# Fills in turned order, a narrow last pair, and a first k product in column halves

## The chip, the cores and the metric

The kernel runs on one core of a Trainium2 chip. A core has five engines that run side by side, each through its own list of instructions: PE (TensorE, matrix products), DVE (VectorE), ACT (ScalarE), POOL (GpSimd) and SP (SyncE, which here only issues transfers). They meet through semaphores. PE writes its products into PSUM, eight banks of 128 partitions by 512 float32 values; everything else lies in SBUF, 128 partitions wide. The metric is the device time of one execution in microseconds (us).

## What is computed

The reference is a transformer block on 2048 tokens of width 512, in float32:

```
h  = x + A(layernorm(x))
h2 = h + B(layernorm(h))

A: q, k, v = heads of x @ wqkv                         (32 heads of 16)
   phi(u)  = [softmax(u @ w_phi), softmax(-u @ w_phi)]
   o       = phi(q) (phi(k)^T v) / (phi(q) . sum(phi(k)) + 1e-6)
   A       = o @ wo
B: (token mixing) u = gelu(layernorm(h)^T @ w1 + b1)   (512 x 1792)
   B = (u @ w2 + b2)^T
```

Both layer norms are without weights; B normalizes its input once more, which the kernel folds into one scale.

## The kernel before

Every large product is made in a split form: an operand is rounded to the fast float32 form (the high part), the rest is the low part, and a product is high x high + high x low + low x high. ACT makes most high parts by a copy, DVE or POOL the low parts by a subtraction (`split`, lines 58 to 61). Tokens go in 16 tiles of 128.

**The beginning (lines 221 to 354)** has its order on PE, DVE, ACT and POOL written out by hand. The k, v and q weights arrive in chunks of 128 output columns: chunks 4 to 7 are k, 8 to 11 v, 0 to 3 q. `center` takes out the mean of a chunk, `fold` multiplies (or transposes) it on PE into PSUM, `hi_w` and `lo_w` (lines 279 to 287) copy it out as high and low part. `hi_w` runs on ACT, or on DVE where its second argument is True. `split_x(t)` makes the two parts of a token tile, the high one on ACT, the low one on POOL. Then `proj` (line 122) makes a tile's k logits in one PSUM bank: for tile 0 with `by_part`, all high x high first (four matmuls of 512 columns, one for each quarter of the contraction), then x low x weight high, then x high x weight low; for the other tiles in turn. DVE's `k_ops` reads the bank (the maximum of a head at line 154, the minimum at 155, the differences at 148 and 152). The centering of chunk 8 stands on DVE behind the low parts of chunks 4 to 7.

**The middle (lines 646 to 698)** runs 19 rounds `it`. A round carries different tiles at different steps: the denominators (POOL's `s_ez`, DVE's `s_den`, POOL's `s_pq` at line 463), the transposed q features (`s_tr`), the products with the k-v state in every second round (`s_num`, line 549), the product with `wo` (`s_wo`), the residual and the moments (`s_h`, `s_moments`), POOL's scale (`s_rstd`, lines 588 and 589) and the normalized tile `HN` with its parts (`s_hn`, line 593, `split` at 60 and 61). In even rounds `s_hn` makes tile `it - 4` near the beginning and tile `it - 3` at the end. `fills(it)` (line 640) already does part of B's first product: `fill(0)` adds tile `it - 5`, `fill(1)` tile `it - 6` to columns 0 to 255 and 256 to 511 of u, six matmuls each (lines 65 to 67). The w1 pairs for them are loaded, copied by ACT (line 612) and split by DVE (line 604) at the end of a round.

**The end (lines 752 to 912).** The rest of B's first product and gelu follow; then B's second product, in 8 pairs of token tiles by 7 steps `p`. A pair of tiles and a pair of contraction blocks make a 2 x 2 product of blocks, done with seven block products in place of eight; `PROD` (line 814) lists the seven: operand of w2, operand of u, PSUM bank, and half of the bank. With a half, `product` (line 818) writes 256 columns with three matmuls (high x high, high x low, low x high). With None it takes the bank whole: one matmul of 512 columns gives high x high in the left and high x low in the right half, and one of 256 adds low x high to the left. Steps 0 to 4 of a pair go step by step; the last two go product by product (`products(sp, [p - 1, p], order)`), so that the banks are complete one after the other. Then ACT and DVE combine the banks into two blocks of 128 x 512. For the last pair (`LAST`, lines 891 to 912) the two blocks, `hb`, are read back from `out`, b2 is added, and 14 DVE additions end in three stores: SP's whole first block, ACT's left and SP's right half of the second. w2 is loaded by SP, summed by DVE, copied by ACT (line 793) and split by DVE (line 802) in groups of two steps.

Tiles come from pools, and dependencies are kept by tile: a reader of a PSUM tile waits until the last matmul into it that precedes the reader in the program. A k or `py` tile is one bank. PE, DVE, ACT and POOL keep the written order in the first part and in the middle, PE, DVE and ACT at the end; between, a scheduler places the instructions.

Of the kernel before, what the change touches and what calls it, by code (L numbers as in the profile page):

```python
# [17 lines left out]
P = 128  # L18
S, D, H, DH, F = 2048, 512, 32, 16, 1792
NT = S // P  # L20
KD = D // P
NF = F // P
NP = NF // 2
HD = D // 2
# [6 lines left out]
LAG = 5  # L31
# [5 lines left out]
def block_kernel(ctx: ExitStack, tc: tile.TileContext, x, xT, wT, phic, wo, w1, b1, w2, b2,  # L37
                 kvmask, ident_in, out):
    nc = tc.nc
# [58 lines left out]
    X, XH, EQ, PK, VS, SQ, PS, W = {}, {}, {}, {}, {}, {}, {}, {}  # L98
# [23 lines left out]
    def proj(t, wh, wl, pool, name, by_part=False):  # L122
        o = pool.tile([P, D], F32, name=name, tag=name)
        if by_part:
            for i, (a, w) in enumerate(((0, wh), (1, wh), (0, wl))):
                for kt in range(KD):
                    nc.tensor.matmul(o, X[t][:, a, kt, :], w[:, kt, :], start=i == 0 and kt == 0,
                                     stop=i == 2 and kt == KD - 1)
            return o
        for kt in range(KD):  # L130
            mm3(o, X[t][:, 0, kt, :], X[t][:, 1, kt, :], wh[:, kt, :], wl[:, kt, :],
                kt == 0, kt == KD - 1)
        return o
# [87 lines left out]
    with tc.tile_pool(name="prep", bufs=1) as prep:  # L221
# [57 lines left out]
        def hi_w(c, vector=False):  # L279
            if vector:  # L280
                nc.vector.tensor_copy(parts(c)[0], FO[c])
            else:
                nc.scalar.activation(parts(c)[0], FO[c], AF.Copy)
# [8 lines left out]
        with tc.manual_schedule(engines={ET.PE, ET.DVE, ET.Activation, ET.Pool}):  # L292

            nc.gpsimd.tensor_mul(ph.rearrange("p c (a f) -> p c a f", f=DH),
                                 pc[:, 0:64].rearrange("p (c f) -> p c f", f=DH).unsqueeze(2).to_broadcast([P, 4, 8, DH]),
                                 pc[:, 64:72].unsqueeze(1).unsqueeze(3).to_broadcast([P, 4, 8, DH]))
            center(4, True)
            center(5, False)
            fold(4, ps_q, "pu")
            center(6, True)  # L300
            fold(5, ps_q, "pu")
            center(7, False)
            fold(6, ps_v, "pv")
            fold(7, ps_v, "pv")
            hi_w(4, True)
            hi_w(5, True)
            hi_w(6)
            split_x(0, xr[0])
            hi_w(7)
            for c in range(4, 8):  # L310
                lo_w(c)
            split_x(1, xr[1])
            k0 = proj(0, wkh, wkl, ps_k, "pk_ps", True)
            center(8, True)
            for c in range(9, 12):
                center(c, False)
            k1 = proj(1, wkh, wkl, ps_k, "pk_ps")
            for c in range(8, 12):
                fold(c, *((ps_q, "pu"), (ps_v, "pv"))[c // 10])
            k_ops(0, k0)  # L320
            split_x(2, xr[2])
            k_ops(1, k1)
            stats_x(0)
            k2 = proj(2, wkh, wkl, ps_k, "pk_ps")
            for c in range(8, 12):
                hi_w(c)
            for c in range(8, 12):
                lo_w(c)
            stats_x(1)
            exps(0, PK[0])  # L330
            split_x(3, xr[3])
            split_x(4, xr[4])
            v0 = proj(0, wvh, wvl, ps_v, "pv")
            k_ops(2, k2)
            stats_x(2)
            k3 = proj(3, wkh, wkl, ps_k, "pk_ps")
            k_norm(0)
            center(0, True)
            v_out(0, v0)
            exps(1, PK[1])  # L340
            center(1, False)
            exps(2, PK[2])
            v1 = proj(1, wvh, wvl, ps_v, "pv")
            k_ops(3, k3)
            fold(0, ps_q, "pu")
            fold(1, ps_q, "pu")
            k_norm(1)
            center(2, False)
            v_out(1, v1)
            hi_w(0)  # L350
            hi_w(1)
            lo_w(0)
            lo_w(1)
            center(3, False)
# [270 lines left out]
    def fill(p, pool=None):  # L625

        t = FN[p]
        FN[p] = t + 1
        if FL[p] <= t:
            fill_load(p)  # L630
        if any(part is WI[p, t - t % 2][1] for part, _, _ in LATER):
            flush()
        if t == 0:
            PU[p] = [pool.tile([P, D], F32, name="pu", tag="pu") for _ in range(2)]
        a, b = WI[p, t - t % 2]
        for c in range(2):
            mm3(PU[p][c], a[:, t % 2, c * P:(c + 1) * P], b[:, t % 2, c * P:(c + 1) * P],
                HN[t][:, 0], HN[t][:, 1], t == 0, t == NT - 1)

    def fills(it):  # L640
        if FN[0] <= it - LAG:
            fill(0, ps_f)
        if FN[1] < it - LAG:
            fill(1, ps_q)

    for it in range(NT + 3):
        even = it % 2 == 0
# [158 lines left out]
    with tc.issue_after(LO[-18]), tc.issue_after(LD[-20]):  # L806
        for i in range(3):
# [5 lines left out]

    PROD = ((2, 1, 0, None), (5, 5, 1, None), (0, 0, 2, 0), (1, 4, 2, 1), (3, 6, 3, None), (6, 2, 4, None),
            (4, 3, 5, None))
    LAST = PROD[:-1] + ((4, 3, 5, 0),)

    def product(o, half, a, b, first, start, stop):
        if half is None:
# [7 lines left out]
    def products(sp, ps, order):  # L827
        for a, b, bk, half in order:
            for p in ps:
                wh_, wl_ = AW[sp, p]  # L830
                product(bank[bk], half, (wh_[:, a], wl_[:, a]), UB[p, b], half != 1, p == 0, p == NP - 1)
# [6 lines left out]
    for n, (sp, p) in enumerate(STEPS):  # L838
# [10 lines left out]
                bank.append(pool.tile([P, 2, HD], F32, name="py", tag="pu"))  # L849
                n_bank += 1  # L850
        order = LAST if last else PROD
        if p < NP - 2:
            products(sp, [p], order)
            continue
        if p < NP - 1:
            continue
        products(sp, [p - 1, p], order)
        e = uo.tile([P, 2, HD], F32, name="e")
        u2 = uo.tile([P, HD], F32, name="u2", bufs=1)
        u3 = uo.tile([P, HD], F32, name="u3")  # L860
# [32 lines left out]
            nc.sync.dma_start(flat(hb[i]), out[(t + i) * P:(t + i + 1) * P, :])  # L893
            nc.vector.tensor_scalar(hb[i], hb[i], b2s[:, t + i:t + i + 1], None, op0=ALU.add)
        nc.scalar.activation(e[:, 1], bank[0][:, 0], AF.Copy)
        nc.vector.tensor_add(e[:, 1], bank[0][:, 1], e[:, 1])
        nc.vector.tensor_add(hb[1][:, 1], e[:, 1], hb[1][:, 1])
        nc.vector.tensor_sub(u2, bank[1][:, 0], e[:, 1])
        nc.vector.tensor_add(u2, bank[1][:, 1], u2)
        nc.vector.tensor_sub(hb[1][:, 0], hb[1][:, 0], u2)  # L900
        nc.vector.tensor_sub(u3, u2, bank[2][:, 0])
        nc.vector.tensor_sub(hb[1][:, 0], hb[1][:, 0], bank[2][:, 1])
        nc.vector.tensor_add(hb[0], hb[0], u3.unsqueeze(1).to_broadcast([P, 2, HD]))
        nc.vector.tensor_add(hb[0][:, 0], bank[2][:, 1], hb[0][:, 0])
        nc.vector.tensor_add(hb[0][:, 1], bank[3][:, 0], hb[0][:, 1])
        nc.vector.tensor_add(hb[0][:, 1], bank[3][:, 1], hb[0][:, 1])
        nc.sync.dma_start(out[t * P:(t + 1) * P, :], flat(hb[0]))
        nc.vector.tensor_add(hb[1][:, 0], bank[4][:, 0], hb[1][:, 0])
        nc.vector.tensor_add(hb[1][:, 0], bank[4][:, 1], hb[1][:, 0])
        nc.scalar.dma_start(out[(t + 1) * P:NT * P, 0:HD], hb[1][:, 0])  # L910
        nc.vector.tensor_add(hb[1][:, 1], bank[5][:, 0], hb[1][:, 1])
        nc.sync.dma_start(out[(t + 1) * P:NT * P, HD:D], hb[1][:, 1])


def _layout(A_x, A_wqkv, A_w_phi, A_wo, B_w1, B_b1, B_w2, B_b2):
# [46 lines left out]
```

## Time and profile before

| | |
|---|---|
| time, median of 3 runs | 529.30 us (529.26 to 529.55) |
| the profiled execution | 529.31 us, span 527.5 us, clock granted 0.999 |
| PE busy | 516.5 us, 98% of the span |
| DVE, ACT, POOL busy | 394.5, 278.3, 246.6 us |
| first instruction of the first k product | 9.92 us |
| stage with the fills | 172.6 to about 269 us |
| last matmul issued | 522.51 us |
| last store issued | 524.77 us |

A timeline row has the start, the duration, the engine and its line, the operation, out<-in, the shape, and in brackets the idle time of the engine before it and who ended it. PEld is PE's weight load, which overlaps its products; SPq and ACTq are issues of transfers. A matmul's duration is longer than the time after which the next one starts, so starts are what to compare. A row with x4 holds four instructions in a row. The list of waits has: who waited for whom, us in total, times, the longest. The chain is what ended last, followed back from the end; a row there has start, duration and what. A row of one line's instructions has the shortest, median and longest duration in ns.

### The profile page before, as it was taken

The page shows a single profiled execution, that of the slowest core. Times are in us where ns is not written, and L with a number is a line of the kernel's source. Part 1 is how long each engine was busy: PE and PEld are TensorE (multiplying, and loading weights), DVE is VectorE, ACT ScalarE, POOL GpSimd, SP SyncE. Part 2 cuts the span into 40 slices and gives each one's busy share as a digit, 9 for nine tenths or more (in the row PEclk, how much of TensorE's full clock was granted, in tenths as well). Part 3 has the DMA queues.
Part 4 walks back from the last instruction along what each step waited for, and adds up shares of the span by engine and source line. Part 5 has one row for each costly group of instructions (what it writes and reads, how often), then busy time and mean ns, then how long its engine had stood idle before and what let it go on. Part 6 is the DMA issues. An engine that isn't in the chain of part 4 may idle for free.

```text
span 527.5 us, 8840 instructions
## 1 busy us (share of the span) xinstructions
PE 516.5 (98%) x3343; PEld 434.1 (82%) x3343; DVE 394.5 (75%) x684; ACT 278.3 (53%) x481; POOL 246.6 (47%) x204
## 2 busy tenths in 40 slices
PE   8999999999999989999999999999999999999996
PEld 7888888887877767777788888888899999999995
DVE  6993999976899989875325523725779888988985
ACT  6999843534247776557746423625453434434430
POOL 2589699985999988887326000000002112111210
PEclk9999999999999999999999999999999999999999
DMA  8743310030122233334234354532215687668742
GB/s 298 203 129 121 84 39 21 1 86 18 49 93 80 91 96 115 109 111 139 85 99 119 99 161 155 166 98 80 69 51 113 160 187 169 135 146 198 141 61 60
DMA packets 36298, 58.52 MB, mean 111 GB/s; under 512 B 3744, under 2 KB 19360, under 8 KB 36256
## 3 DMA queue, kind: packets, MB, share of 16 engines
q1 hardware_dynamic: 31936, 51.37, 31.2%
q0 software_dynamic: 4032, 6.42, 9.6%
q8 instruction: 26, 0.43, 0.4%
q10 hardware_dynamic: 288, 0.17, 0.1%
q14 instruction: 16, 0.13, 0.1%
HBM read 46.81 MB, written 11.14 MB: 110 GB/s over the span
## 4 chain that ended last, share of the span: by engine, by line
PE 80%; POOL 12%; DVE 4%; ACT 2%; DMA 1%; issue 0%; DVEq 0%; POOLq 0%; ACTq 0%
PE py L820 12%; PE pu L65 11%; PE pu L66 10%; PE pu L67 10%; PE py L824 8%; PE py L821 6%; POOL ez L445 4%; POOL eq L463 3%; PE pv L66 3%; PE pv L67 3%; PE pv L65 3%; PE pk_ps L65 2%; PE pk_ps L67 2%; PE pk_ps L66 2%; POOL hs L61 2%; PE kvp L210 2%
## 5 line engine op out<-in xcount | busy, mean ns | idle before, releaser
L604 DVE TENSOR_TENSOR wlo<-wraw,whi 128x512 fp32r<-128x512 f32 x56 | 50.6, 908 | 54.6 <-ACT whi L612 53.4
L66 PE MATMUL pu<-hs,whi 128*128 128x512 f32 x224 | 87.6, 391 | 2.1 <-POOL hs L61 2.1
L65 PE MATMUL pu<-hs,whi 128*128 128x512 f32 x224 | 87.5, 395 | 0.0
L67 PE MATMUL pu<-hs,wlo 128*128 128x512 f32 x224 | 87.3, 390 | 0.0
L878 POOL DMA_DIRECT2D out<-ot x7 | 6.2, 889 | 149.1 <-DVE ot L874 149.1
L793 ACT ACTIVATE whi<-wraw 128x1792 fp32r<-128x1792 f32 x28 | 47.4, 1701 | 46.7 <-PE py L820 20.6
L820 PE MATMUL py<-uf,whi 128*128 128x512 f32 x195 | 70.9, 399 | 0.0
L802 DVE TENSOR_TENSOR wlo<-wraw,whi 128x1792 fp32r<-128x1792 f32 x28 | 56.5, 2022 | 12.0 <-PE py L821 8.9
L612 ACT ACTIVATE whi<-wraw 128x512 fp32r<-128x512 f32 x56 | 34.9, 626 | 47.3 <-PE pu L66 43.0
L821 PE MATMUL py<-uf,wlo 128*128 128x256 f32 x195 | 54.9, 282 | 0.0
L66 PEld LDWEIGHTS pu<-hs,whi 128*128 128x128 f32 x224 | 42.1, 188 | 11.5 <-POOL hs L61 3.1
L65 PEld LDWEIGHTS pu<-hs,whi 128*128 128x128 f32 x224 | 42.1, 188 | 10.8 <-issue 2.5
L67 PEld LDWEIGHTS pu<-hs,wlo 128*128 128x128 f32 x224 | 42.1, 188 | 9.0 <-DVE wlo L604 0.4
L820 PEld LDWEIGHTS py<-uf,whi 128*128 128x128 f32 x195 | 36.8, 189 | 7.3
L445 POOL TENSOR_TENSOR ez<-eq,zB 128x1024 f32<-128x1024 f32 x16 | 40.6, 2539 | 4.4 <-ACT zB L492 4.4
L821 PEld LDWEIGHTS py<-uf,wlo 128*128 128x128 f32 x195 | 36.9, 189 | 0.0
L198 POOL TENSOR_TENSOR pk<-pk,sk 128x1024 f32<-128x1024 f32 x16 | 31.0, 1943 | 7.9 <-DVE sk L197 5.3
L463 POOL TENSOR_TENSOR eq<-eq,w 128x1024 f32<-128x1024 f32 x16 | 31.9, 1997 | 1.2 <-DVE w L460 1.2
L824 PE MATMUL py<-uf,whi 128*128 128x256 f32 x170 | 32.0, 283 | 0.0
L202 POOL TENSOR_TENSOR zacc<-zacc,pk 128x1024 f32<-128x1024 f32 x13 | 31.2, 2402 | 0.5
L61 POOL TENSOR_TENSOR hs<-hn,hs 128x512 fp32r<-128x512 f32 x16 | 21.4, 1337 | 17.8 <-ACT hs L60 17.8
L820 PE MATMUL py<-un,whi 128*128 128x512 f32 x78 | 28.8, 399 | 0.0
(183 smaller groups left out, 1317.8 us busy)
## 6 DMA issues: line engine op xcount, KB each, us to landing
wraw<-in_w SPq DMA_DIRECT2D x56, 256.0 KB, 2.8
wraw<-in_w SPq DMA_DIRECT2D x28, 512.0 KB, 4.4
xraw<-in_xT SPq DMA_DIRECT2D x16, 256.0 KB, 2.9
xh<-in_x SPq DMA_DIRECT2D x16, 256.0 KB, 2.7
h<-in_x SPq DMA_DIRECT2D x16, 256.0 KB, 3.0
out<-h SPq DMA_DIRECT2D x16, 256.0 KB, 3.0
out<-ot POOLq DMA_DIRECT2D x14, 256.0 KB, 4.5
wraw<-in_wT SPq DMA_DIRECT2D x12, 256.0 KB, 5.2
```

Source lines behind the costliest of these rows:

```text
L65: nc.tensor.matmul(o, ah, bh, start=first, stop=False)
L66: nc.tensor.matmul(o, ah, bl, start=False, stop=False)
L67: nc.tensor.matmul(o, al, bh, start=False, stop=last)
L445: nc.gpsimd.tensor_mul(EZ[t], EQ[t], zB)
L463: nc.gpsimd.tensor_mul(heads(EQ[t]), heads(EQ[t]), W[t].rearrange("p g c h -> p (g c h)").unsqueeze(2).to_broadcast([P, 2 * H, DH]))
L604: LO.append(nc.vector.tensor_sub(wl_, raw, wh_).ins)
L612: nc.scalar.activation(wh_, raw, AF.Copy)
L793: nc.scalar.activation(WH[g], RAW[g], AF.Copy)
L802: nc.vector.tensor_sub(wl_, RAW[g], WH[g])
L820: nc.tensor.matmul(o, a[0], b, start=start, stop=stop, skip_group_check=True)
L821: nc.tensor.matmul(o[:, 0], a[1], b[:, 0], start=False, stop=stop, skip_group_check=True)
L824: nc.tensor.matmul(o[:, half], a[x], b[:, y], start=start and first and i == 0, stop=stop and i == 2, skip_group_check=True)
```

## The change

Four edits. The first k product takes its high x high part and its weight-low part in halves of 256 columns, the x-low part stays whole; 20 matmuls in place of 12. The copy of chunk 6's high part goes from ACT to DVE. In `fills`, fill 1 is written ahead of fill 0. In the last pair all seven products are half products, so they fill three and a half banks in place of six; the last three steps, not two, run product by product; and the combination has ten DVE additions in place of 14, since no half of high x low products is left to be added.

```diff
     def proj(t, wh, wl, pool, name, by_part=False):
         o = pool.tile([P, D], F32, name=name, tag=name)
         if by_part:
-            for i, (a, w) in enumerate(((0, wh), (1, wh), (0, wl))):
+            half, whole = [slice(0, D // 2), slice(D // 2, D)], slice(0, D)
+            turn = [(0, wh, half[0]), (0, wh, half[1]), (1, wh, whole), (0, wl, half[0]), (0, wl, half[1])]
+            for i, (a, w, cols) in enumerate(turn):
                 for kt in range(KD):
-                    nc.tensor.matmul(o, X[t][:, a, kt, :], w[:, kt, :], start=i == 0 and kt == 0,
-                                     stop=i == 2 and kt == KD - 1)
+                    nc.tensor.matmul(o[:, cols], X[t][:, a, kt, :], w[:, kt, cols], start=i == 0 and kt == 0,
+                                     stop=i >= 3 and kt == KD - 1, skip_group_check=True)
...
             hi_w(5, True)
-            hi_w(6)
+            hi_w(6, True)
             split_x(0, xr[0])
...
     def fills(it):
+        if FN[1] < it - LAG:
+            fill(1, ps_q)
         if FN[0] <= it - LAG:
             fill(0, ps_f)
-        if FN[1] < it - LAG:
-            fill(1, ps_q)
...
-    LAST = PROD[:-1] + ((4, 3, 5, 0),)
+    LAST = ((2, 1, 0, 0), (5, 5, 0, 1), (0, 0, 1, 0), (1, 4, 1, 1), (3, 6, 2, 0), (6, 2, 2, 1), (4, 3, 3, 0))
...
         order = LAST if last else PROD
-        if p < NP - 2:
+        run_on = 3 if last else 2
+        if p < NP - run_on:
             products(sp, [p], order)
             continue
         if p < NP - 1:
             continue
-        products(sp, [p - 1, p], order)
+        products(sp, range(NP - run_on, NP), order)
...
         nc.scalar.activation(e[:, 1], bank[0][:, 0], AF.Copy)
-        nc.vector.tensor_add(e[:, 1], bank[0][:, 1], e[:, 1])
-        nc.vector.tensor_add(hb[1][:, 1], e[:, 1], hb[1][:, 1])
-        nc.vector.tensor_sub(u2, bank[1][:, 0], e[:, 1])
-        nc.vector.tensor_add(u2, bank[1][:, 1], u2)
+        nc.vector.tensor_add(hb[1][:, 1], bank[0][:, 0], hb[1][:, 1])
+        nc.vector.tensor_sub(u2, bank[0][:, 1], e[:, 1])
         nc.vector.tensor_sub(hb[1][:, 0], hb[1][:, 0], u2)
-        nc.vector.tensor_sub(u3, u2, bank[2][:, 0])
-        nc.vector.tensor_sub(hb[1][:, 0], hb[1][:, 0], bank[2][:, 1])
+        nc.vector.tensor_sub(u3, u2, bank[1][:, 0])
         nc.vector.tensor_add(hb[0], hb[0], u3.unsqueeze(1).to_broadcast([P, 2, HD]))
-        nc.vector.tensor_add(hb[0][:, 0], bank[2][:, 1], hb[0][:, 0])
-        nc.vector.tensor_add(hb[0][:, 1], bank[3][:, 0], hb[0][:, 1])
-        nc.vector.tensor_add(hb[0][:, 1], bank[3][:, 1], hb[0][:, 1])
+        nc.vector.tensor_add(hb[0][:, 0], bank[1][:, 1], hb[0][:, 0])
+        nc.vector.tensor_sub(hb[1][:, 0], hb[1][:, 0], bank[1][:, 1])
+        nc.vector.tensor_add(hb[0][:, 1], bank[2][:, 0], hb[0][:, 1])
         nc.sync.dma_start(out[t * P:(t + 1) * P, :], flat(hb[0]))
-        nc.vector.tensor_add(hb[1][:, 0], bank[4][:, 0], hb[1][:, 0])
-        nc.vector.tensor_add(hb[1][:, 0], bank[4][:, 1], hb[1][:, 0])
-        nc.scalar.dma_start(out[(t + 1) * P:NT * P, 0:HD], hb[1][:, 0])
-        nc.vector.tensor_add(hb[1][:, 1], bank[5][:, 0], hb[1][:, 1])
-        nc.sync.dma_start(out[(t + 1) * P:NT * P, HD:D], hb[1][:, 1])
+        for k, o, q in ((0, bank[2][:, 1], nc.scalar), (1, bank[3][:, 0], nc.sync)):
+            nc.vector.tensor_add(hb[1][:, k], o, hb[1][:, k])
+            q.dma_start(out[(t + 1) * P:NT * P, k * HD:(k + 1) * HD], hb[1][:, k])
```

In the built programs the order on PE differs further near 275 us (a few fills' matmuls trade places, by the scheduler), and one pair on ACT near 267 us (line 585 and line 612) trades places; the orders on POOL and SP are the same, and DVE's differs only by the copy and the end.

## The prediction

> **What bounds the kernel now.** I read the page's chain by engine first, then the waits of PE, then the chain and the timeline at the three places that the change touches: the first k product (7 to 21 us), the stage with the fills (165 to 240 us), the last pair of token blocks (505 us to the end).
>
> ```profile
> span 527.5 us, 8840 instructions
> PE 80%; POOL 12%; DVE 4%; ACT 2%; DMA 1%; issue 0%; DVEq 0%; POOLq 0%; ACTq 0%
> ```
>
> ```profile
> PE pu L66 <- POOL hs L61: 2.1, 3, 1.0
> PE tn L549 <- ACT pht L532: 1.6, 2, 1.4
> ```
>
> PE carries four fifths of the end time and hardly waits: the list holds five groups, these two and three of the first 10 us. So a step pays if it shortens PE's own work, a wait of PE in a stage where PE sets the end, or what comes before PE's first and after its last matmul. The 12% of POOL is one stretch, the fill stage; there PE's waits are an effect of POOL.
>
> **The last pair (predicted gain 1.36 us).** The end, by the timeline:
>
> ```profile
> 518.23 0.28 PE L821 MATMUL py<-uf,wlo 128*128 128x256 f32 x1
> ...
> 518.55 0.38 ACT L895 ACTIVATE e<-py 128x256 f32<-128x256 f32 x1 [7.32 <-PE py L821]
> ...
> 518.97 0.42 DVE L896 TENSOR_TENSOR e<-py,e 128x256 f32<-128x256 f32 x1 [3.22 <-ACT e L895]
> ...
> 519.43 0.42 DVE L897 TENSOR_TENSOR hb<-e,hb 128x256 f32<-128x256 f32 x1
> ...
> 519.77 0.42 DVE L898 TENSOR_TENSOR u<-py,e 128x256 f32<-128x256 f32 x1
> ...
> 521.68 0.69 DVE L903 TENSOR_TENSOR hb<-hb,u 128x512 f32<-128x512 f32 x1
> ...
> 522.51 0.28 PE L824 MATMUL py<-uf,wlo 128*128 128x256 f32 x1
> ...
> 523.65 0.34 SPq L907 DMA_DIRECT2D out<-hb  x1
> ...
> 524.33 0.41 DVE L911 TENSOR_TENSOR hb<-py,hb 128x256 f32<-128x256 f32 x1
> 524.44 0.35 ACTq L910 DMA_DIRECT2D out<-hb  x1
> 524.77 0.34 SPq L912 DMA_DIRECT2D out<-hb  x1
> ```
>
> The reader is to see that PE is done at 522.51 + 0.28 = 522.79, while VectorE, back to back since 518.97, ends at 524.74 and lets the last store go at 524.77. For the last 6 us the end is set by VectorE's 14 additions, which could not begin before the first bank was complete (518.51, ACT's copy at 518.55). The change attacks this twice: narrow products leave one bank half each in place of two, so four additions go; and three steps run product by product in place of two, so the banks are complete earlier and further apart.
>
> What PE pays: seven steps have four wide products each, so 28 times a 512-column and a 256-column matmul become three of 256.
>
> ```profile
> 501.61 0.40 PE L824 MATMUL py<-uf,whi 128*128 128x256 f32 x2
> ...
> 503.05 0.41 PE L820 MATMUL py<-uf,whi 128*128 128x512 f32 x1
> ...
> 504.47 0.40 PE L820 MATMUL py<-uf,whi 128*128 128x512 f32 x1
> ```
>
> Four triples take 501.61 to 503.05, 0.360 us each; four pairs 503.05 to 504.47, 0.355. So 28 x 0.005 = 0.14 us more; with two-digit starts the difference is good to 0.003, so 0.06 to 0.22. [...]
>
> PE then ends at 522.93. A dependency here is kept by tile, and a tile is a bank, so a bank is released when both its products are in. With 0.36 x 3 = 1.08 us per product, bank 3 (one product) is complete at 522.93, bank 2 at 521.85, bank 1 at 519.69, bank 0 at 517.53. VectorE needs 0.34 us from one addition to the next where they are independent (519.43 to 519.77) and 0.46 where one reads the other's result (518.97 to 519.43); the wide one 0.72. So: ACT's copy 517.57 to 517.96; first addition 517.98, u2 518.32, the third 518.78, then it waits; u3 at 519.73, the wide one 520.19, two more 520.91 and 521.25, then it waits; bank 2 at 521.89 and 522.23, the first store goes at 522.36, ACT's at 522.68; the last addition at 522.97, the last store at 523.41. Before: 524.77. Gain 1.36 us. VectorE now idles in front of each bank: PE ends the kernel.
>
> Behind the last store lie 527.5 - 524.77 = 2.7 us before; first and last store were 1.12 us apart, now 1.05, so I leave this term alone. ACT's half store now leads by 0.73 where it led by 0.33: up to 0.4 us could come off if the two shared bandwidth. From the other side, an added wait of PE could eat it: the narrow steps reach the last pair's low parts earlier.
>
> ```profile
> 512.93 2.02 DVE L802 TENSOR_TENSOR wlo<-wraw,whi 128x1792 fp32r<-128x1792 f32 x1 [1.64 <-PE py L824]
> ...
> 515.15 0.39 PE L820 MATMUL py<-uf,whi 128*128 128x512 f32 x1
> ```
>
> They are ready at 514.95. Step p = 4 began at 515.15; now step 5's first low-part matmul follows 0.6 us later, at 515.8. That leaves 0.8 us, and the two VectorE additions of b2 come after it: free. SP's loads of the two blocks, and POOL's stores of the pair before, are issued where they were. The term's bounds: 1.1 to 1.8.
>
> **The first k product (predicted gain 0.3 us).**
>
> ```profile
> 6.76 1.31 DVE L281 CAST wkh<-pu 128x512 fp32r<-128x512 f32 x2
> ...
> 7.17 2.03 PE L271 MATMUL pv<-ph,wraw 128*128 128x128 f32 x16
> 7.27 0.72 ACT L265 ACTIVATE wraw<-wraw,mu 128x512 f32<-128x512 f32 x1
> 7.98 1.28 DVE L287 TENSOR_TENSOR wkl<-pu,wkh 128x512 fp32r<-128x512 f32 x2
> ...
> 8.27 0.60 ACT L283 ACTIVATE wkh<-pv 128x512 fp32r<-128x512 f32 x1 [0.27 <-PE pv L271]
> 8.76 0.62 ACT L60 ACTIVATE xs<-xraw 128x512 fp32r<-128x512 f32 x1
> ...
> 9.28 0.59 ACT L283 ACTIVATE wkh<-pv 128x512 fp32r<-128x512 f32 x1
> 9.46 2.54 POOL L61 TENSOR_TENSOR xs<-xraw,xs 128x512 fp32r<-128x512 f32 x2 [4.57 <-ACT xs L60]
> ...
> 9.92 2.11 PE L127 MATMUL pk_ps<-wkh,xs 128*128 128x512 f32 x8 [0.71 <-ACT wkh L283]
> ...
> 11.41 0.88 DVE L261 TENSOR_SCALAR wraw<-wraw,mu 128x512 f32<-128x512 f32 x1
> ...
> 12.98 0.69 DVE L154 TENSOR_REDUCE mx<-pk_ps 128x32 f32<-128x512 f32 x1 [0.69 <-PE pk_ps L127]
> ...
> 15.70 0.69 DVE L154 TENSOR_REDUCE mx<-pk_ps 128x32 f32<-128x512 f32 x1 [0.24 <-PE pk_ps L67]
> ```
>
> ACT loses one copy of 0.60, so the x split moves from 8.76 to about 7.9 and POOL's part of it from 9.46 to 8.6. The fourth chunk's copy still waits for its transposed product (7.17 + 2.03 = 9.20): 9.24 to 9.83, nearly as before. PE now starts the left half, which needs the chunks that VectorE had done at 8.07, at about 9.2, four half matmuls (0.48 us) before the right half at 9.88. From there right half, POOL part and low part take 0.1 + 0.48 + 4 x 0.23 + 0.96 = 2.46: the last issue ends at 12.34 where it ended at 9.92 + 12 x 0.23 + 0.1 = 12.78. PE is 0.44 us earlier.
>
> VectorE pays: its copy waits for chunk 6 (8.27, by ACT's wait) and takes 0.60 from issue to issue (0.655 by the CAST row), so the four low parts start at 8.87 in place of 7.98, and the centering after them 0.76 us later (11.27 for 10.51). It had 0.69 us of idle time before the first maximum and 0.24 before the second. If L261 still takes 0.88, the first maximum starts at about 13.0, as before, and the second at 15.4: 0.3 earlier, all of VectorE's slack. If L261 takes less, because POOL's subtractions are over by then, the bound is PE: 0.44. Behind it stand the v low parts and v's second matmul, which had waited for VectorE at 20.69; they move with VectorE. I take 0.3; bounds 0 (a longer wait for chunk 6) to 0.44.
>
> Does it reach the end? From 20.7 to 152 us the chain is PE's alone, and its list of waits has none there. At 165 us POOL takes over, and it waits there for a chain that came through PE and VectorE:
>
> ```profile
> 165.00 0.55 POOL L588 TENSOR_TENSOR r<-ve,mhalf 128x1 f32<-128x1 f32 x1 [0.68 <-ACT ve L585]
> ```
>
> 0.68 us of idle time is enough to pass 0.3 on.
>
> **The fills turned (predicted gain 0).** In an odd round fill 0 takes the newest normalized block, whose low part POOL is just writing; fill 1 takes one a round older.
>
> ```profile
> 186.84 0.50 PE L66 MATMUL pu<-hs,whi 128*128 128x512 f32 x1 [0.98 <-POOL hs L61]
> ...
> 194.98 1.10 PE L549 MATMUL tn<-pht,kvB 64*32 64x256 f32 x32 [1.42 <-ACT pht L532]
> ```
>
> With fill 1 ahead, six matmuls (1.4 us) stand in front of that wait, and all 2.1 us of it go. What is late next is the s_num product L549: it already waits 1.42 at 194.98 and 0.21 at 239.08 for ACT's copy, which stands behind POOL. The chain there:
>
> ```profile
> 232.43 2.81 POOL ez L445
> ...
> 236.05 0.83 ACT hn L593
> ...
> 238.06 0.97 ACT pht L532 x2
> ...
> 239.08 1.05 PE tn L549 x25
> ```
>
> Nothing in it comes from a fill. So PE arrives earlier and waits longer at L549, and 239.08, from where PE runs without a wait to the end, stays. The other wait, for wlo, is not made worse: in an even round fill 1 opens a pair whose low part was made a round earlier. ACT's swapped pair (moment, copy) near 267 us and PE's order near 275 us lie where PE waits for nothing: 0.
>
> **Sum.** The profiled execution took 529.31 us, 1.8 outside its span; the median is 529.30. 529.31 - 1.36 - 0.30 = 527.65, a span of 525.8; against the median 527.6.
>
> **Rivals.** (a) The fills do pay: the 2.1 us that PE waits come out, because PE's earlier arrival moves the s_wo products and through them VectorE, ACT and POOL. For it: PE reaches L549 only 0.21 early at 239.08. Against it: POOL's own chain. 525.5 us.
> (b) Slower: POOL's long products stretch. A product of the fill stage takes one of two lengths:
>
> ```profile
> L445 POOL TENSOR_TENSOR ez<-eq,zB x16: 2381/2406/2850, 128.9 to 232.4; 128x1024 f32<-128x1024 f32 x16
> ```
>
> 0.45 us apart, and POOL is the chain there. When PE runs earlier, VectorE's work shifts against POOL's; four long ones more eat the 1.66 us, seven give 529.3 - 1.66 + 3.1 = 530.8 and make it slower. [...] Against (b): PE's waits at L549 keep VectorE where it was.
> (c) VectorE takes the whole front gain: 0, the tail alone: 527.9.
> (d) The narrow pair does not do what it says: stores closer together or a wait per bank give the tail's gain back. From 0.6 us lost the sum is within 0.2% of before; about 528.7.
>
> **How the numbers follow.** Forecast (527 to 528.2, with c) 0.66; (a) or part of it 0.11; (d) 0.14; (b) 0.09. Faster by over 0.2%, about what a measurement here can tell from no change (below 528.2): forecast, a and little of (d), 0.78; within: 0.14; slower: 0.08. The range reaches half way to (a) and to just under before's time: 526.4 to 529.1.
>
> **What would show it.** Right: the last store about 0.6 us behind PE's last matmul (before 2.3), VectorE waiting for PE at u3, at the first block's right half and at the last addition; first k matmul at 9.2; L66's wait for hs gone and L549's grown; L549 near 239 us earlier by 0.3 only. Wrong: POOL's long products more often at 2.8 us, a PE wait for wlo after 515, the first maximum later than 13.1, or the stage from 165 to 239 us shorter by more than 0.5.

## The result, and the profile after

The changed kernel takes 527.96 us (median of 10 runs, 527.32 to 528.90) where the kernel before takes 529.57 (10 runs). The ratio is 0.9969, with a 95% interval of 0.9961 to 0.9977: faster by 1.6 us. The forecast was 527.6. The profiled execution took 527.88 us, 1.43 less than that of before (529.31), and the parts below are taken from these two.

First the page of the changed kernel, and two groups from its list of waits (lines here are those of the kernel before plus two):

```profile
span 526.1 us, 8910 instructions
PE 82%; POOL 12%; DVE 3%; ACT 2%; issue 0%; POOLq 0%; ACTq 0%
```

```profile
PE tn L551 <- ACT pht L534: 3.8, 2, 2.8
PE po L65 <- DVE h L579: 0.8, 1, 0.8
```

PE's wait of 2.1 us for the normalized block's low part is gone. The wait at the s_num product grew by 2.2 us, and a new one of 0.8 us stands at the s_wo product: PE now waits 4.6 us in this stage where it waited 3.7. The s_num product near the end of the stage, by the timeline:

```profile
194.84 1.10 PE L551 MATMUL tn<-pht,kvB 64*32 64x256 f32 x32 [2.77 <-ACT pht L534]
...
238.98 1.10 PE L551 MATMUL tn<-pht,kvB 64*32 64x256 f32 x32 [1.07 <-ACT pht L534]
```

It starts at 238.98 where it started at 239.08. Then the tail, by the timeline:

```profile
517.52 0.38 ACT L898 ACTIVATE e<-py 128x256 f32<-128x256 f32 x1 [6.39 <-PE py L826]
...
519.68 0.42 DVE L902 TENSOR_TENSOR u<-u,py 128x256 f32<-128x256 f32 x1 [0.53 <-PE py L826]
...
521.84 0.42 DVE L906 TENSOR_TENSOR hb<-py,hb 128x256 f32<-128x256 f32 x1 [0.23 <-PE py L826]
...
522.60 0.28 PE L826 MATMUL py<-uf,wlo 128*128 128x256 f32 x1
...
522.92 0.42 DVE L909 TENSOR_TENSOR hb<-py,hb 128x256 f32<-128x256 f32 x1 [0.32 <-PE py L826]
523.37 0.34 SPq L910 DMA_DIRECT2D out<-hb  x1
```

VectorE now idles ahead of each bank. The last store is issued 0.77 us behind the start of PE's last matmul, where it was 2.26. And the front:

```profile
5.18 2.47 PE L273 MATMUL pu<-ph,wraw 128*128 128x128 f32 x16
...
7.49 1.95 PE L273 MATMUL pv<-ph,wraw 128*128 128x128 f32 x16
...
9.20 0.72 PE L129 MATMUL pk_ps<-wkh,xs 128*128 128x256 f32 x4
...
10.13 1.67 PE L129 MATMUL pk_ps<-wkh,xs 128*128 128x256 f32 x8 [0.22 <-ACT wkh L285]
...
12.48 0.49 DVE L263 TENSOR_SCALAR wraw<-wraw,mu 128x512 f32<-128x512 f32 x1
...
12.89 0.68 DVE L156 TENSOR_REDUCE mx<-pk_ps 128x32 f32<-128x512 f32 x1
...
20.53 0.50 PE L66 MATMUL pv<-wvl,xs 128*128 128x512 f32 x1
```

The first k matmul starts at 9.20 as forecast, but fold's last matmul ends at 7.49 + 1.95 = 9.44 where it ended at 9.20 before, and the right half begins at 10.13 and not at 9.88. Two starts serve as marks below, tile 0's second v matmul (20.53, the last row) and the first `py` matmul:

| us | before | after | difference |
|---|---|---|---|
| fold's last matmul ends | 9.20 | 9.44 | +0.24 |
| from there to tile 0's second v matmul | 11.49 | 11.09 | -0.40 |
| from there to the first `py` matmul | 362.66 | 362.74 | +0.07 |
| from there to the start of PE's last matmul | 139.153 | 139.338 | +0.185 |
| from there to the last store's issue | 2.26 | 0.77 | -1.49 |

Up to rounding the sum is the 1.40 us by which the last store is earlier (524.77 to 523.37); the other 0.03 lies behind it. The tail gave 1.3 net, the front 0.4, of which a later fold took 0.24 in this execution, and the fills gave nothing here.

### The profile page after: what moved, and what is told of

Same layout as the page of the kernel before. It is cut to its first block, busy times and chain, and to the rows that moved or that the text cites. A ratio compares the mean times of both kernels' runs of the same rounds, so it can differ in the third digit from the quotient of the medians.

```text
span 526.1 us, 8910 instructions
## 1 busy us (share of the span) xinstructions
PE 516.9 (98%) x3379; PEld 436.5 (83%) x3379; DVE 394.0 (75%) x681; ACT 277.7 (53%) x480; POOL 245.2 (47%) x204
## 4 chain that ended last, share of the span: by engine, by line
PE 82%; POOL 12%; DVE 3%; ACT 2%; issue 0%; POOLq 0%; ACTq 0%
PE py L822 11%; PE pu L65 11%; PE pu L66 10%; PE pu L67 10%; PE py L826 10%; PE py L823 6%; POOL ez L447 4%; POOL eq L465 3%; PE pv L66 3%; PE pv L67 3%; PE pv L65 3%; PE pk_ps L65 2%; PE pk_ps L66 2%; PE pk_ps L67 2%; POOL hs L61 2%; PE kvp L212 2%
## 5 line engine op out<-in xcount | busy, mean ns | idle before, releaser
L822 PE MATMUL py<-uf,whi 128*128 128x512 f32 x175 | 63.4, 399 | 0.0
L65 PEld LDWEIGHTS pu<-hs,whi 128*128 128x128 f32 x224 | 42.1, 188 | 10.8 <-issue 2.5
L823 PE MATMUL py<-uf,wlo 128*128 128x256 f32 x175 | 49.2, 281 | 0.0
L826 PE MATMUL py<-uf,whi 128*128 128x256 f32 x210 | 39.0, 283 | 0.0
L822 PEld LDWEIGHTS py<-uf,whi 128*128 128x128 f32 x175 | 33.0, 188 | 6.8
L826 PEld LDWEIGHTS py<-uf,whi 128*128 128x128 f32 x210 | 32.4, 189 | 1.4
L823 PEld LDWEIGHTS py<-uf,wlo 128*128 128x128 f32 x175 | 33.1, 189 | 0.0
```

The source lines that it names most:

```text
L65: nc.tensor.matmul(o, ah, bh, start=first, stop=False)
L822: nc.tensor.matmul(o, a[0], b, start=start, stop=stop, skip_group_check=True)
L823: nc.tensor.matmul(o[:, 0], a[1], b[:, 0], start=False, stop=stop, skip_group_check=True)
L826: nc.tensor.matmul(o[:, half], a[x], b[:, y], start=start and first and i == 0, stop=stop and i == 2, skip_group_check=True)
```

## Experiments

Times are medians; a ratio is to the kernel before, with its 95% interval.

### The parts one at a time

**The narrow last pair alone.** The hunks of `LAST`, `run_on` and the additions, on the kernel before.

```diff
-        if p < NP - 2:
+        run_on = 3 if last else 2
+        if p < NP - run_on:
...
+    LAST = ((2, 1, 0, 0), (5, 5, 0, 1), (0, 0, 1, 0), (1, 4, 1, 1), (3, 6, 2, 0), (6, 2, 2, 1), (4, 3, 3, 0))
```

> The kernel before with the narrow last pair alone (half products, three steps run on, ten additions). Theory (the end was VectorE's chain of 14 additions behind a late first bank; now PE's last bank sets it): last store about 0.6 us behind PE's last matmul, 1.4 us earlier than before, PE's last matmul 0.1 to 0.2 us later; about 528.1 us, ratio 0.9974. Rival (narrow steps and closer stores give part back): over 528.6 us, ratio above 0.9985.

Measured: 528.28 us, ratio 0.9977 (0.9967 to 0.9986). PE takes 139.34 us from its first to its last `py` matmul (0.185 more), and the last store follows 0.77 behind:

```profile
522.86 0.28 PE L824 MATMUL py<-uf,wlo 128*128 128x256 f32 x1
522.89 0.35 ACTq L908 DMA_DIRECT2D out<-hb  x1
523.18 0.42 DVE L907 TENSOR_TENSOR hb<-py,hb 128x256 f32<-128x256 f32 x1 [0.32 <-PE py L824]
523.63 0.34 SPq L908 DMA_DIRECT2D out<-hb  x1
```

The tail carries about 1.2 us of the change's 1.6; the interval just touches the rival's ratios (above 0.9985), but the trace has both terms as the theory gave them.

**The first k product in halves, with VectorE's copy.**

```diff
-            hi_w(6)
+            hi_w(6, True)
...
+            turn = [(0, wh, half[0]), (0, wh, half[1]), (1, wh, whole), (0, wl, half[0]), (0, wl, half[1])]
```

> The kernel before with the first k product in halves and VectorE's copy of chunk 6 alone. In the changed kernel's trace PE's matmuls came 0.21 us apart until 6.15 us and 0.11 after, in the kernel before until 4.19 us; nothing that the change moves lies so early. Theory G (the late step of PE's rate took part of the front's gain): if PE's rate doubles before 5 us here, fold ends near 9.0 us and tile 0's v product starts 0.3 us or more earlier than 20.68; if it doubles near 6 us, 0.16. Rival (VectorE's chain alone took the gain): 0.16 whatever the time of the step. Either way the end moves 0.1 to 0.4 us: 529.1 to 529.4, ratio 0.9993 to 0.9998.

Measured: 528.99 us, ratio 0.9990 (0.9981 to 0.9999). PE's rate doubled at 6.55 us, fold ended at 9.73, and the second v matmul came at 20.82: later than before's 20.69, so neither expectation holds as written. Read from the end of fold it is 11.09 us, as in the changed kernel, against 11.49 before. The series on the front below takes this up.

**The fills turned, alone.**

```diff
     def fills(it):
+        if FN[1] < it - LAG:
+            fill(1, ps_q)
         if FN[0] <= it - LAG:
             fill(0, ps_f)
-        if FN[1] < it - LAG:
-            fill(1, ps_q)
```

> The kernel before with fill 1 ahead of fill 0 alone. Theory (POOL's chain sets the stage): no change, ratio 1.000 within 0.001; PE's 2.1 us wait for the normalized block's low part gone, its wait for ACT's transposed features at the s_num product grown from 1.6 to 3.7 us, that product at 239.0 as before. Rival (fills pay): 2.1 us off, 527.4, ratio 0.996.

Measured: 529.24 us, ratio 0.9997 (0.9988 to 1.0006): no change that can be seen. From its list of waits:

```profile
PE tn L549 <- ACT pht L532: 3.8, 2, 2.8
...
PE po L65 <- DVE h L577: 0.7, 1, 0.7
```

The wait moved and did not shrink, as expected. The rival's 2.1 us are excluded. What PE's rate did about such a longer single wait, 2.8 us where it was 1.4, is taken up with the fill stage below.

### The tail: half products or a third step run on?

The change puts two things into the tail. Each was tried without the other.

**Two steps run on, narrow products kept** (on the changed kernel):

```diff
-        run_on = 3 if last else 2
+        run_on = 2
```

> The changed kernel with the last two steps, not three, run product by product in the last pair. Theory: with 0.36 x 2 = 0.72 us per product the first bank is complete near 519.3 and not 517.5, so VectorE is back to back from there: last addition near 523.6, last store near 524.0 against 523.37, so 0.65 us slower than the changed kernel: 528.6 us, ratio 0.9981. Rival (the end hangs on PE alone, and four additions fewer were enough): as the changed kernel, ratio 0.997.

**Three steps run on, wide products and 14 additions kept** (on the kernel before):

```diff
-        if p < NP - 2:
+        run_on = 3 if last else 2
+        if p < NP - run_on:
...
-        products(sp, [p - 1, p], order)
+        products(sp, range(NP - run_on, NP), order)
```

> The kernel before with three steps, not two, run product by product in the last pair, wide products and 14 additions kept. Worked out by 1.07 us per product: first bank complete near 516.3 and not 518.5, so the 14 additions begin 2.2 us earlier and the last one only waits for the last bank at 522.8: last store near 523.4, 1.4 us earlier, as in the changed kernel, ratio 0.9973. Rival (the dropped additions carry the gain): last store not before 524.1, ratio above 0.9985.

The last rows of the timeline, first with two steps and narrow products:

```profile
519.99 0.38 ACT L898 ACTIVATE e<-py 128x256 f32<-128x256 f32 x1 [8.18 <-PE py L826]
...
523.27 0.28 PE L826 MATMUL py<-uf,wlo 128*128 128x256 f32 x1
...
523.72 0.75 DVE L909 TENSOR_TENSOR hb<-py,hb 128x256 f32<-128x256 f32 x2
...
524.49 0.34 SPq L910 DMA_DIRECT2D out<-hb  x1
```

then with three steps and wide products:

```profile
517.29 0.38 ACT L896 ACTIVATE e<-py 128x256 f32<-128x256 f32 x1 [5.18 <-PE py L821]
...
520.51 0.42 DVE L902 TENSOR_TENSOR u<-u,py 128x256 f32<-128x256 f32 x1 [0.67 <-PE py L824]
...
524.26 0.34 SPq L913 DMA_DIRECT2D out<-hb  x1
```

| | last store behind the start of PE's last matmul | PE from its first to its last `py` matmul | time, ratio |
|---|---|---|---|
| before: two steps, wide | 2.26 | 139.153 | 529.57 |
| two steps, narrow | 1.22 | 139.337 | 529.26, 0.9988 (0.9979 to 0.9996) |
| three steps, wide | 0.87 | 139.152 | 528.31, 0.9974 (0.9965 to 0.9984) |
| after: three steps, narrow | 0.77 | 139.338 | 527.96, 0.9969 (0.9961 to 0.9977) |

The last column is not to be read down: both narrow kernels of this table also have the new front and the turned fills. On the kernel before, the narrow pair alone took 528.28 us (0.9977) and the wide pair with three steps 528.31 (0.9974), which the times can't tell apart, so what follows rests on the traces. Running a third step on takes 1.39 of the 1.49 us by itself, at no price on PE. The half products then take 0.10 more off VectorE's end, which with wide products runs without a pause from 520.51 on, and cost PE 0.185: in the changed kernel they lose 0.09 us. Only with two steps do they pay, 1.04 less 0.185. (The wide kernel's own last store is at 524.26 because in that execution a weight chunk came late, VectorE waiting 1.47 us for it where it waited 0.28 in the kernel before, and fold ended at 10.01; the measure from PE's last matmul is free of that.) With two steps and narrow products the tail costs 0.45 against the changed kernel, where 0.65 was expected, and three stores 0.33 us apart are followed by 3.1 us of span where 2.7 us follow in the changed kernel. That makes 0.78. The two profiled executions are 1.45 apart; the rest is 0.50 that PE lost in the fill stage to a lower granted clock (0.82 from 193 to 212 us where the changed kernel has 1.00; next part) and 0.17 of a later front. The medians are 1.3 apart, and most of its runs had that lower clock: seven of eleven (0.994 to 0.996) took 528.91 to 529.41 us, the other four 528.14 to 528.69.

### Who sets the fill stage?

Six of POOL's low parts go to VectorE, one round later, on the changed kernel:

```diff
+        if later:
+            nc.scalar.activation(HN[t][:, 0], hn, AF.Copy)
+            HL_.append((HN[t][:, 1], hn, HN[t][:, 0]))
+            return
         split(HN[t][:, 0], HN[t][:, 1], hn, nc.gpsimd)
...
+        while HL_ and not even:
+            nc.vector.tensor_sub(*HL_.pop(0))
         flush()
...
-            s_hn(it - 3)
+            s_hn(it - 3, 3 < it < 15)
```

> The changed kernel with six of POOL's low parts of normalized tiles (the one at the end of each even round from 4 to 14, 1.27 us each, with 1.59 us of POOL idle before it) made by VectorE in the round after. Theory (POOL's chain sets the stage from 165 to 239 us, PE only waits for it): PE's waits there (2.8 and 1.1 at the s_num product, 0.8 at the s_wo product, 4.6 us together) go, the s_num product of 239.0 comes 3 to 4.6 us earlier: 523.5 to 525 us. Rival (PE's or VectorE's own work sets it; VectorE is busy 12 to 13.5 us of 14): less than 0.5 us off, or slower.

Measured: 523.66 us, ratio 0.9887 (0.9872 to 0.9902): 4.3 us below the changed kernel and 5.9 below the kernel before. Three views of it: the list of waits, the chain from 193 to 240 us by line, and the lengths of POOL's long product (shortest, median, longest in ns).

```profile
PE pu L67 <- DVE wlo L612: 0.6, 1, 0.6
PE tn L551 <- ACT pht L534: 0.4, 1, 0.4
```

```profile
by line: PE pu L65 15.3%; PE pu L66 13.7%; PE pu L67 13.6%; PE po L67 12.6%; PE po L66 12.6%; PE po L65 12.6%; PE tn L532 11.2%; PE tn L551 8.9%; issue 0.1%
```

```profile
L447 POOL TENSOR_TENSOR ez<-eq,zB x16: 2383/2396/2415, 128.5 to 225.9; 128x1024 f32<-128x1024 f32 x16
```

In the changed kernel the chain by line, from 193 to 239 us, reads:

```profile
by line: POOL ez L447 34.7%; POOL eq L465 25.7%; POOL hs L61 16.5%; POOL r L590 8.6%; ACT hn L595 5.4%; ACT hs L60 4.2%; POOL ve L591 2.5%; ACT pht L534 2.1%; issue 1.5%; ACT whi L614 1.1%; PE tn L551 0.9%; POOLq L61 0.2%
```

POOL is gone from the chain of the relieved kernel, PE's waits fell from 4.6 to 1.0 us, and the s_num product of 238.98 starts at 234.81. So POOL did set the stage, and the end of the kernel follows it: from tile 0's second v matmul to the first `py` matmul it takes 358.79 us and not 362.74. (The waits listed account for 3.6 of these 3.95 us; the rest was not followed up.) The lengths show something on the side: none of POOL's sixteen products takes 2.85 us any more, all lie within 2.38 and 2.42. In each of the eleven profiles without the relief five of the sixteen are long, and just these five start while VectorE is in a w1 low part, 0.58 to 0.60 us before that ends; in the relieved kernels none starts so. The two go together; which makes which was not tried. It gives POOL 2.3 us (40.62 to 38.33), beside the six subtractions that it no longer makes.

The same relief with the fills in their old order:

```diff
     def fills(it):
-        if FN[1] < it - LAG:
-            fill(1, ps_q)
         if FN[0] <= it - LAG:
             fill(0, ps_f)
+        if FN[1] < it - LAG:
+            fill(1, ps_q)
```

> The same relief of POOL with fill 0 ahead of fill 1, as before. Theory: with POOL no longer last, a wait of PE in the stage costs its own length; if PE still waits 0.6 to 1 us per odd round for the low part that POOL writes, this is slower than the turned one by up to 2.1 us; if POOL is now early enough, the two are equal. Rival (the order never matters, the stage hangs on neither): equal, with the waits for the low part still there.

Measured: 524.61 us, ratio 0.9905 (0.9892 to 0.9919), 0.95 us above the turned one; by the trace 0.83 of it lies between tile 0's second v matmul and the first `py` matmul. The wait that costs it:

```profile
PE pu L66 <- DVE hs L698: 1.2, 1, 1.2
```

It is one wait, for a low part that VectorE now makes, and not POOL's as expected. But the theory's point holds: once PE sets the stage, turning the fills is worth about what PE waits. In the kernel as it was changed POOL's chain sets the stage, and the turn only moves PE's wait to another place.

One execution shows the same from the other side. In the profile of the narrow pair with two steps PE fell behind near 195 us and made most of it up:

```profile
194.97 1.96 PE L551 MATMUL tn<-pht,kvB 64*32 64x256 f32 x32 [2.77 <-ACT pht L534]
...
211.75 1.09 PE L551 MATMUL tn<-pht,kvB 64*32 64x256 f32 x32
...
239.66 1.10 PE L551 MATMUL tn<-pht,kvB 64*32 64x256 f32 x32
```

At 211.75 PE is 2.9 us behind the changed kernel (208.81), at 239.66 only 0.7 (238.98): it made up 2.2 us by not waiting.

It fell behind because its clock was halved: the 32 matmuls at 194.97 take 1.96 us where they take 1.10 in the changed kernel. Two views by stretches, the first of this kernel, the second of the changed kernel with one warming matmul (next part), which shows the same behind the same wait:

```profile
190.87:194.28 3.41, 1.33 (x6) 0.75 (x4) 3.24 (x8) 3.38 (x6) 2.33 (x2) 1.00 0.31 77
194.28:201.11 6.83, 6.14 (x42) 4.05 (x43) 5.40 (x7) 5.34 (x13) 6.75 (x6) 0.50 0.42 122
```

```profile
193.09:196.50 3.41, 0.77 (x32) 0.50 (x32) 3.38 (x4) 3.38 (x8) 3.41 (x3) 1.00 0.45 121
196.50:199.91 3.41, 3.41 (x23) 2.37 (x8) 2.42 (x5) 1.90 (x6) 3.33 (x4) 0.50 0.53 179
```

(The columns are stretch, length, busy time of PE, weight loads, VectorE, ScalarE and GpSimd with their instructions, granted clock, DMA share, GB/s.) The clock falls 0.7 us before the end of that wait in the first and 0.8 us behind it in the second. It is the wait that turning the fills made longer, 2.8 and 2.7 us here for 1.4. No other profile has such a fall ahead of PE's last matmul (from 100 to 240 us the granted clock of the other twelve is 1.00). Over whole executions the mean granted clock is 0.996 or less in 14 of the 32 executions of the three kernels with the fills turned and POOL not relieved (changed kernel 4 of 10, fills alone 3 of 11, two steps 7 of 11). In 85 executions of kernels with the old order and POOL not relieved it is never below 0.997, in the 12 of the relieved kernels never below 0.999. (A mean of 0.997 decides nothing: with one warming matmul it holds one fall, with the halves alone it comes from the time after PE's last matmul.) So lower clocks came with the fills turned, and the half rate itself (0.50) stands in the two profiles above. What it costs is less clear. In the changed kernel the four executions with 0.996 or less took 528.32 to 528.90 us and the other six 527.32 to 528.02; with the fills alone the three took 529.14 to 529.17, no longer than the rest. The changed kernel with the fills in their old order was not run, so the cost of the turn there is not shown.

### The front: what did the halves and the copy each give?

**Halves alone**, ACT keeping chunk 6:

```diff
-            for i, (a, w) in enumerate(((0, wh), (1, wh), (0, wl))):
+            turn = [(0, wh, half[0]), (0, wh, half[1]), (1, wh, whole), (0, wl, half[0]), (0, wl, half[1])]
+            for i, (a, w, cols) in enumerate(turn):
```

> The kernel before with the first k product in halves alone; ACT keeps chunk 6. Left half at 9.4 (behind ACT's high part of x), right half at 9.95, the x-low part held by POOL until 10.75 (0.3 us of wait); VectorE's low parts 0.6 us earlier than in the changed kernel. Tile 0's v product 0.2 us earlier than before, against 0.16 to 0.3 with both: the copy on VectorE adds at most 0.1. Rival: without the earlier x split nothing is gained, v product at 20.7 to 20.8.

**The copy alone**, the product whole:

```diff
-            hi_w(6)
+            hi_w(6, True)
```

> The kernel before with chunk 6's copy on VectorE alone, the first k product whole. It still waits for ACT's copy of chunk 7 (first k matmul 0.6 us behind the end of fold), and VectorE's 0.65 us go into its idle 0.69 before the first maximum: tile 0's v product 10.7 to 10.8 us behind the first k matmul, as in the kernel before (20.69 - 9.92 = 10.77). Rival: the earlier x split pays by itself, 10.5 or less.

**One warming matmul in place of nine**, on the changed kernel and on the kernel before:

```diff
-        for _ in range(WARM):
+        for _ in range(1):
             nc.tensor.matmul(warm, ones, ones, start=True, stop=True)
```

> The changed kernel with one warming matmul in place of nine. Theory G (PE's rate doubles only after some us of work, and in the new front what comes after hangs on the end of fold): fold runs at 0.21 us a matmul for longer and ends at 10.5 to 12 in place of 9.3, the right half 0.9 us behind it, tile 0's v product 10.4 us behind the right half, so 21.8 to 23.5. Rival (the front hangs on VectorE): v product within 0.3 of 20.53.

> The kernel before with one warming matmul in place of nine: first k matmul 0.6 to 0.9 us behind the end of fold (10.5 to 12), tile 0's v product 10.77 behind that. With the same end of fold the changed front is 0.3 to 0.5 us earlier (theory), or equal (rival: VectorE's chain takes the gain).

These four kernels ran once each, so only the front of their profiles is read. The profiles of all kernels, by which front they have. Fold's end is the end of its last matmul; the rate's step is where its matmuls go from 0.21 us apart to 0.11:

| front, kernel profiled | rate's step | fold's end | tile 0's second v matmul | from fold's end |
|---|---|---|---|---|
| old: before | 4.19 | 9.20 | 20.69 | 11.49 |
| old: narrow pair alone | 5.33 | 9.37 | 20.82 | 11.45 |
| old: three steps, wide | 5.36 | 10.01 | 21.56 | 11.55 |
| old: fills alone | 5.96 | 9.24 | 20.82 | 11.58 |
| old: one warming matmul | 10.77 | 11.71 | 23.28 | 11.57 |
| copy alone | 5.54 | 9.41 | 20.86 | 11.45 |
| halves alone | 6.59 | 9.67 | 21.26 | 11.59 |
| new: relieved | 5.69 | 9.21 | 20.29 | 11.08 |
| new: relieved, four steps, wide | 5.55 | 9.28 | 20.36 | 11.08 |
| new: after | 6.15 | 9.44 | 20.53 | 11.09 |
| new: relieved, fills unturned | 6.50 | 9.56 | 20.65 | 11.09 |
| new: narrow, two steps | 6.53 | 9.61 | 20.70 | 11.09 |
| new: front alone | 6.55 | 9.73 | 20.82 | 11.09 |
| new: one warming matmul | 8.86 | 10.80 | 21.89 | 11.09 |

Every new front takes 11.08 or 11.09 us from fold's end, over 1.6 us of different ends; every old one 11.45 to 11.58. So the front's gain is 0.36 to 0.50 us at the same end of fold, and when fold ends is a matter of the execution. With the same end as before, 9.21, the relieved kernel's second v matmul is at 20.29: 0.40 earlier than 20.69. The changed kernel with one warming matmul came at 21.89, in the theory's stretch (21.8 to 23.5) and 1.4 us behind 20.53, where the rival allowed 0.3; between the two kernels with one warming matmul the front differs by 0.48, in the theory's 0.3 to 0.5.

Neither part gives anything alone. With the copy alone, the whole product still waits for chunk 7, as expected: it starts 0.69 us behind fold's end, and the v matmul 10.8 behind that. Halves alone were expected to gain 0.2 us and gain nothing either; the first product starts at 9.98, not 9.4:

```profile
9.98 2.55 PE L129 MATMUL pk_ps<-wkh,xs 128*128 128x256 f32 x12 [0.31 <-ACT xs L60]
10.00 2.54 POOL L61 TENSOR_TENSOR xs<-xraw,xs 128x512 fp32r<-128x512 f32 x2 [5.25 <-ACT xs L60]
...
12.36 1.11 PE L129 MATMUL pk_ps<-wkl,xs 128*128 128x256 f32 x8
...
21.26 0.50 PE L66 MATMUL pv<-wvl,xs 128*128 128x512 f32 x1
```

The left half has to wait for ACT's high part of x, and then the product for POOL's low part, which starts at 10.00 where the changed kernel has it at 8.56. The copy on VectorE is what brings the x split forward; the halves are what can use it.

### A version that should have been better

The relieved kernel with wide products and four steps run on:

```diff
-        run_on = 3 if last else 2
+        run_on = 4 if last else 2
...
+    LAST = PROD[:-1] + ((4, 3, 5, 0),)
```

> The relieved kernel with wide products and 14 additions in the last pair, four steps run on product by product. Theory (running on carries the tail's gain, the half products cost PE 0.185 us and save nothing more): PE's last matmul 0.18 us earlier, last store 0.8 to 0.9 us behind it: 523.5 us, 0.1 to 0.2 below the relieved kernel. Rival (the four additions less are needed): last store over 1.0 us behind, 523.8 or more.

Measured: 524.94 us, ratio 0.9911 (0.9894 to 0.9927): 1.3 us slower than the relieved kernel, a miss. The timeline:

```profile
508.72 2.03 DVE L812 TENSOR_TENSOR wlo<-wraw,whi 128x1792 fp32r<-128x1792 f32 x1 [1.64 <-PE py L834]
...
510.80 0.39 PE L831 MATMUL py<-uf,wlo 128*128 128x256 f32 x1 [1.25 <-DVE wlo L812]
```

The last store came 0.77 us behind PE's last matmul, as the theory had it. But the fourth step reaches the last pair's low parts before VectorE has made them, and PE waits 1.25 us there (from its first to its last `py` matmul it takes 1.51 more than the other wide kernels, 1.33 more than the relieved one). This is the cover that the prediction put at 0.8 us with three steps run on; the fourth uses it up. Wide products with three steps on the relieved kernel, by the table of the tail 0.09 us better, were not run.

## Why the prediction was right

**The last pair: right.** 1.36 us was forecast. Its own terms were measured as a gain of 1.49 behind PE's last matmul and 0.185 that PE pays, 1.30 net; the 1.40 by which the last store is earlier holds 0.09 from ahead of the first `py` matmul too. The 0.185 are for 28 more matmuls, where 0.14 was read from two-digit starts (bounds 0.06 to 0.22): 6.6 ns for each. All six profiled kernels with narrow products and no wait in them show 139.337 or 139.338 us where the wide ones show 139.152 or 139.153. The four instructions that wait for a bank started at 517.52, 519.68, 521.84 and 522.92; worked out were 517.57, 519.73, 521.89 and 522.97. The last store followed the start of PE's last matmul by 0.77; the prediction's sum has 523.41 - 522.65 = 0.76, and its sign of "about 0.6" does not come out of that sum. What was wrong is the credit: the prediction says that the change attacks VectorE's chain twice. One of the two does it, the third step run on; the narrow products cost more than they add to it.

**The first k product: mechanism right, size off.** The term of 0.3 us was taken as VectorE's bound, because the centering was to keep its 0.88 us. It took 0.49 (the row at 12.48), since POOL's second subtraction of that front was over by then, at 11.98. The other profiles fit: it takes 0.88 in the kernel before, where it shares 0.59 us with that subtraction, 0.65 with the narrow pair alone, where it shares 0.36, and 0.49 wherever it comes after it. That is the case for which the prediction named PE's bound of 0.44, and 0.40 came. In the two profiles only 0.16 of it shows, and with the 0.07 lost in between, 0.09 at the first `py` matmul; the reason is no step of the change but fold's end, 0.24 us later here, which the prediction had taken as given (9.20). The two misses, 0.06 too much at the tail and 0.10 too little here, nearly cancel in the sum.

**The fills: right in the profiled execution, with a risk overlooked.** PE's wait went to the s_num product, as said, and the product at 239 moved by 0.1. That PE's clock falls to 0.50 about the longer wait, as in two profiles, is in none of the rivals. The six runs of the changed kernel with a mean clock of 0.997 or more have a median of 527.63 us, the forecast's 527.6; the 0.3 by which the median of all ten lies above it comes with the other four, and that it comes from the clock alone is not shown. Rival (a), 2.1 us, fell with the fills alone (ratio 0.9997). Its condition was shown by the relief: it would have needed POOL out of the way.

**The other rivals.** (b) fell: POOL's sixteen long products take 40.62 us in all, before 40.63. (c) fell: VectorE did not take the front's gain in any of the seven profiles of the new front. (d) fell in the changed kernel. Part of what it named, closer stores that end later, may stand in the kernel with two steps (3.1 us behind the last store), which was seen in one profile.

## What to carry to other kernels

A wait of the busiest engine is worth nothing while another engine's chain sets the stage; move a piece of that chain first (six subtractions of 1.3 us gave 4.3 us here), and only then does the order on the busy engine pay. Two waits put together into one longer wait may even hurt: here PE ran at half its rate about it in two profiles (granted clock 0.50 for 6.83 and for 3.41 us). Where a result is combined at the end, spread the completion of its parts before making the combination cheaper: with a third step run on product by product, the half products and the four additions fewer were worth no more than they cost. But each step run on reaches its operands sooner, and the cover on them has to be counted: three steps had it, with the fourth PE waited 1.25 us.

## What the hardware showed

PE's rate at the start is not the same in two executions. Its first matmul starts at 1.06 us, and its nine warming matmuls (two records each) took, in the kernel before and in the changed one:

```profile
1.06 3.74 PE L291 MATMUL pk_ps<-ones 128*128 128x128 f32 x18 [1.06 <-DVE eps L56]
```

```profile
1.06 4.21 PE L293 MATMUL pk_ps<-ones 128*128 128x128 f32 x18 [1.06 <-DVE eps L56]
```

The starts are 0.21 us apart at first and 0.11 later; the step lies at 4.19 us in one and at 6.15 in the other, and between 4.19 and 6.59 over the kernels with nine warming matmuls, while the granted clock that the profile gives for these stretches reads 1.00 all the same; it is the starts that show the rate. With one warming matmul it lies at 8.86 and 10.77, that is 3.5 and 5.4 us after fold begins. In the kernels with nine it comes 3.1 to 5.5 us after PE's first matmul (1.06). What sets its time is not shown.

In the two falls of the fill stage the granted clock shows the half rate: 0.50 for 6.83 us in the kernel with two steps, where the 32 matmuls of the s_num product take 1.96 us for 1.10, and 0.50 for 3.41 us in the changed kernel with one warming matmul. The wait alone does not bring it: the changed kernel has the same wait, 2.77 us up to 194.84, and its granted clock stays at 1.00 up to there and behind:

```profile
190.00:194.84 4.84, 2.07 (x11) 1.38 (x9) 4.67 (x9) 4.55 (x8) 3.21 (x3) 1.00 0.20 73
194.84:204.00 9.16, 9.16 (x72) 7.31 (x73) 7.95 (x14) 6.38 (x15) 9.08 (x7) 1.00 0.36 115
```

What brings a fall is not shown.

With nine warming matmuls fold ended between 9.20 and 9.73 us (leaving out the one with the late chunk), a spread as large as the front's gain; the step's time is one reason for it, fold's start (5.06 to 5.37) another.
